# A ResNet block on one Trainium2 core: another written-out order of the same instructions, and nine more constant matmuls in its opening

## The chip, the core and the metric

The kernel runs on one core of a Trainium2 chip. The metric is the device time of one execution in microseconds (us); the number of the kernel before is the median of three runs. The profile is of one further execution, with its own time. The engines are TensorE (PE, with its weight loads PEld beside it), VectorE (DVE), ScalarE (ACT), GpSimd (POOL) and SyncE (SP), which issues most DMAs.

## What is computed

```python
B, C, HW, E = 2, 512, 64, 1152
h = conv3(_silu(gn(x, g1, be1)), w1)        # group norm of 4 groups, silu, 3x3 convolution 512 -> 512
emb = _silu(t_emb) @ w_emb
h = h + emb.reshape(B, C, 1, 1)
h = conv3(_silu(gn(h, g2, be2)), w2)
return x + h
```

Everything comes in and goes out in bfloat16. x is 2 x 512 x 64 x 64.

## The kernel before

The 512 channels are four blocks of 128 partitions (ct). An image is split into two chunks of rows, so that two layers, two images and two chunks give eight chunks, c = 0 to 7. Chunks 0 and 1 are image 0 in layer 1, 2 and 3 image 1 in layer 1, 4 to 7 the same in layer 2. A chunk has four units, one for each block of output channels: `u20` is chunk 2, output block 0. The convolution is done with transformed rows: for a chunk, `silu` (ACT) normalises and activates a block, `k`, `row` and `rob` (`rows_a`, `rows_b`; DVE with some ACT) form the planes of transformed rows, PE multiplies them by transformed weights into PSUM, ACT copies PSUM out (`o`, `m`, `b` in names), DVE recombines (`S`, `A`, `s`, `d`, `y`). The planes of chunk c+1 are formed while the units of chunk c run. So at the start of a chunk PE needs the last planes that DVE made (`rob13`, `rob23`, `rob33`, `rob53`, `rob63`).

Group norm of layer 2 is folded: `gn2_0` and `gn2_1` are chains of small DVE operations with one small matmul group in them; they use PSUM bank 7, which a `p5` group of a unit uses next. `emb` is a chain of its own: five matmul groups (`emb.0` to `emb.4`) each behind its load, then a DVE copy from PSUM (L1105).

**The opening.** Chunk 0 needs the statistics of x first. For each block ct, `stats0` (named `st0ct` below) takes the half x[0,ct,0] (`x0ct`) and the half x[0,ct,1] (`x1ct`). Block 0 uses four batch-norm statistics on DVE (L1125) for one half; blocks 1 to 3 use PE for it: eight matmuls of ones (128x260) and a Gram matrix of 17 matmuls (128x128), whose diagonal DVE sums (L1194). For the other half, each block has eight ones matmuls on PE and a square on ACT (2.1 us with its accumulator), and ACT reads the ones' sums from PSUM. Then `gn_chain` (L452 on) has a small group of fp32 matmuls, some DVE operations and a power on POOL, and gives scale and bias. Then `silu0ct`, `k0ct`, `row0ct`, and PE begins the convolution with the groups `o.0` to `o.23` (three 128x512 matmuls each): `o.6ct` to `o.6ct+5` are those of block ct. After them come the units `u00`, `u01`, and so on.

Two PE groups compute nothing that is used: `warm` is 11 matmuls of a constant tile of ones (128x512) in one step, and `fill` is a list of steps with one such matmul each. Both write PSUM bank 5 and depend on nothing but that bank:

```python
mm([(Ps(5, 0, [[1, 512]]), cone, wide, True, True) for _ in range(CFG["warm"])], "warm", chain=False, ...)
for i in range(CFG["fill"]):
    mm([(Ps(5, 0, [[1, 512]]), cone, wide, True, True)], "fill", chain=False, slack=0.0, slow=1.0)
```

**What sets the order.** `Plan.op` records each step with its engine, a cost, and the steps it depends on. `Plan.emit(ORDER)` then issues the steps in the order that the string ORDER spells (two characters for a step). Each engine runs its steps in the order in which they are issued, and so does each DMA queue; semaphores carry the dependencies. PE steps of the convolution are chained in program order; the statistics, `emb`, `gn2`, `warm` and `fill` (`chain=False`) may stand anywhere among them that their dependencies allow. Stores of the units wait for GpSimd's accumulating DMAs (`oa`), loads stand in SP's queue between such stores.

Of the kernel before, what the change touches and what calls it, by code (L numbers as in the profile page):

```python
# [165 lines left out]


ORDER = (
    "0E09000B0A2T0C0G0F0D0c010H020304050607080b0I160a130R0Z140X0g0S0Y150d0f0e0T0h1817190i0j0U0k1A0l1B0K1C2M1D0m0n1u0L"
    "0o2J0V0W1E0v0M1N1X3C1F0O1G1Y0p1Z0y0J1r0r1a3K1b1_0q1H201Q0N1c2c221d0s211e1I0t1f23241g4g0_1h3E251J0u2U261i271j0w28"  # L170
    "1K291k3F0x100Q0z120-2A3D1L1l2B1M1m1O1n2C4L111P1o1R2f1S4T3H1p2D1q1x2F1s3L2E1t1y1v2G1w1T2e2P2H2i2I3G2K1U2Q1-2L0P2N"
    "2W2O1V2X1z2l2Y1W2m3g2V2Z2R2n2b4O2h2d2o2S2p3a2a2q3X4N2r3M2s3N3h2g4M2t3i3O2u3P2v4U2k2w2x3Q2j2y3R2_2z3S3Z3j3d2-3k3u"
    "303T5P323v3U4V313w4Q3J5H4X3x4W3y3I3V3z4P333-4Y3_343l374Z423c3m3543366L3W443Y4a453b465J4S4h4k4738485K5Q493e394q3r"
    "4b3n4r3o4e4B4s5I4c4t4R3f4u4m4v406D4n4A4w414x4f4j6Y4-5R4_4d6M505T3p6Z513q525L6a535U547u556F5V5S5c4l3s5X4i5d7v5e4C"
    "6E5f7w5h5W5i4D4G4o5jB74EB85k4p3A4F5l5M4H5m5n3t5Z4I5Y5o566G8y575r4z6N5s4y5a5tB9583B5u5b5w6P5x595C5N5y6O5A6Q5z5BBB"
    "5-5v6RBN8z5_5g7h6S6I605D616b4J6T5E6H6c6U6d8l8-6e6XBA6W6g5q6h6iBFBCBP6j6kBD5p6l6mA06n626sBO6VBG636t6JBE5O6KA14K6u"
    "A25F6vB46x646y6w6z6-65686_7071BRBH727666B5BJ6777D56f6978DDBQ7PBIBT796A6o7Q6pBS7A7RB6DE737BBU7S6r5G7TBL7CBK7D7UBM"
    "7V7W7x7X747Y7Z7y7aD67E7b6q7z7c7F7d75DG7-7eDF7f7G80D781827gDH7i8384D985Ee86DJ87DL8C7H8DDI7I7j8E7JD27K8F7l888H7k8G"
    "8I8J8K8m7m8L8M8ND39p8O7n8S7L8T897p8U6B7M7_7o8VDN8A8W8Q7q8a8XD4D88n8Y8PDB8Z8o8_8bDA8p909qDMDC7r918q928BAt947s6C95"
    "9697988r998R9ADK9B9G7t7O8c9HEf8s9IDP9J8tEm9L8d9M9N9O8w8f9P9Q9R8e9S8x9W8g8u9XEg8h939Y9C9ZDOEi8i9D9r9aEuEh9F7N9bAu"  # L180
    "DR9cDQ9s9d9tA39UEn8vA49K9u9TA59ECr9e9vA69V9fA89xA9A7AA8jAB9gACAD9wAE9kAFAK9hAGAHAL9y9jAMEkEoAvAN9iEjAPEpAQAxElCs"
    "ARAS9-ATAUAVAWAa9lEvAbDS9zAX9mAcAyAYAdAw8kAeAzEO9_AfAIA_AgAiA-AhAJBVAjB09nBWEwAZCtBXB3AkBYB2BaBbAoBcAlBdAOBeBfCv"
    "AnBgBhBlCuAmBmBnBjBoApBiBtBZBuBpCwAqBkBvEyBq9oBwEbGJB1ByBzCQEqB-B_CREcC0GBC1CxExC2CTEdC3BxC6CUCzC7C8C4C9EsCCCAEr"
    "CDC5CyEtAsCEE-CVC-CFFxEzDTBrGLDUC_GDGKE_CGDVCSBsEPCWD1DWGCD0DYDZDaDbCBDcDdDgDeDfGFEQDjCXCHDkDlCYG8DmDrGNDhCZCIDs"
    "HhGECaGRG9DtCKCbERGMDuCLCJCcESDwFyDxDyCdGADzD-CeETD_E0E1CME4HUE5E6DoE7DnEAGHDiCNCfEBDXEUArGPE2ECGGDvEVEDGSHjEWF0"
    "GTCgGOE3F1GIChE8EXF2DqFzF3CiDpGQF5CjEaF6F7GVF8F9EEE9FAHpFBFCFEFGHVHlFHFIFJEFHxFOEYHiFPCkF_GUFQEGFLFREZEIFTEJFUEH"
    "FVG0FWFFFXFYF4GWFZFaEKFDFdFeHrFfFgHkFjG1FKELClGXFkFbF-HqFSFlGYJ6FMFcFmHtFhCOG2GZCPCmHnGaCnHmGbG3GcHzFNHyI3FnG5Ge"
    "GfJ7GgHsG7GhGiG4GnGjGmGkGlFiHWGpJ8GqHoGrGsHuGxFoEMGyHvGuKNGoGzFpGtCpG-HYI4FrHwFsH0G6H1H2ENH3H4CoHZH5H6H7FqHAHaHB"
    "FtHCHDH-HGG_HXFuHHGdGwKPHII5KOHbHEHJCqHcI6IBH9GvHKICHdNMH8IDHgJ9HfIENLIGHFIHIIIJIKI7ILIMHLINIRIQISH_ITHPIUHMIZIP"
    "I0IOIaHOHNI9IbIWI1IVIcIFI8I2HeIeJAIfHQIgIhFvIiIjIkIlIXHRIoInIpJCIqIAIdIrIuIYImJDIvIsJBIwJEItKQIxJGJSJLJFJTJUJHIy"  # L190
    "JJJVKRJXJYJZIzJaJbJcI-FwJdMvJeLeJiKTJjLfJkJlJIJqKSJ0JrKUOzI_JsJ1JKJtLgJfMxO-J2KVJvJwJgJxJhJyMwKXJzJ-JWJ_KWK0JnK3"
    "K4JuJMK5K6JmKbK9K1KYKAK2KaK7KBLhKCKZKjKcJNKkJoKDKlJ3LiKmJpJOKoKpKqK8KrKsKnKtKuLkKvKxKzMyJPK-HSK_L0KEL5LlL6LjLmL7"
    "KFKIOiL8OjKwJQLAKHNHNGLBLoLCKGLDLELnQBLFKyLGJRLHHTLKLLOkLpNJLMLNLQLrLROxL1L2KJLSMzQALTLsL-L4L_L9M_LIM0M-LJM1N0Pv"
    "LUM3L3PwM4LOM5KdM6N1M7M8LPM9J5MAJ4MEMFKeMGMHLVMMLqNKMCMNMDLWMOLZKKLXMPN2MBKLMRLYMSKfMTMUM2MVN3MWMJMXPxLtMIMYLaMb"
    "KMMcMdMeMhN6MiMQMLMjMZN4MkMaMKNNMfN7NOMlOyKgOlNPMgN8NQOHN5NSNTMmNUNVOmNWLbNXNYNZOIKhNbMnNcMqOKOnNdMoOoR5RMMpNFNe"
    "KiLdNgNhMrQ8NiNjNkNlNmOpLcNnNRNrNsMsNtOqNuNvLuNaNwQ9NxNyOrMuN-OLLvN_O0O1OsO2O3O4LwO5O_NfOMOJLxNoP0ONOwP1NzNpP2Nq"
    "O6P4OtP5P6PyP7O7OOP8P9PAOPPBLyPDO8PzPELzPFRKO9PGN9OAR7PIR6P-PJOCPKPLNAOBPMPNP3POOvPPMtPTPCPUPVPWP_PXPQPYPZRLODPa"
    "PcPHPdPePfQ0PgOEPhPiSZPRPjQ1QCPSOFPkQDOuTlPbQESHNINBQFQ3R8QHPlSIQIOGQJQKQLQMQ2QNQOQQPmNCQRPqPnQSQ5PoQTQ4PpQVSXQW"
    "QPQXQ7QYQZQ6QaR9QbQcQgSJQhTkQiNDQjQkQlPrQmQGQnQpQURNQqQrRBPtQoQsQtQuRAQvQwQdPsRCROSYNERPRDQeQxRQRERRW7SKRFRTPuRU"
    "QfRVRWRXRGSWRYTTRZRaRJSLRcRHRdTVRIReTiUfRfSNRhRiSMRjW6RkSORlRmRnQyRoSPRsRtRbUhRuTjRvSRRwRxRSRyQzRzR_TUS0SQR1S1S2"  # L200
    "S3Q-S4S5S6SUR0UgSaQ_SbRgSSScRpXJR2SdSfSVR-R3SgShOQSiORSjS7OSRqSkSlSmOTRrSoOUSpS8SnSqOVS9SrR4OWSASDStUvSuSvOXSwSB"
    "OYSxOZSyOaSCSzObSTS-T2UwS_T3OcT4OdT5OeOgT6OfSeT7OhSET8TWT9TBUuTCTDTET1SFTFTGTHT0TITmTATnTJToTXTpTKTrTsTtTLTuTvSs"
    "TwVrTZTxSGTyT-TzTaT_TYTbU0TMVsUiU1TcTdU3U4UxU5TPU6TeU7TNU8U9TfTOVtUAUEUFUjTgUGUHUIUJUKThULW4UNUOTqTQUPX1UQUBURUS"
    "W5UTUlUUTRUyUMUkUzUVUmU-UDX2UnU_UCU2V1UpVuV2V3V4UoV5V6TSV7UWX3V8VAVBUqVCUXXGVvUtVDUYVFVGVHUsVIUZYFVJVKV9VLVMUbVQ"
    "VxVRVNVSVTVwVUVVUaVWVyYDVXVZVEVaUcYEVbVzVcVdV0VeVfUrUdVgVYW8ZnVPW9VhV-WAV_X4WBVOXIWDW0WEWFWGViWHWIX5WJWKWMW2WNVj"
    "YGWOZUb0X7WPVkXHWRWSX6WTWLWUWVW1YVWWZSUeWXWYVmVnWcX8WdVlWeZmWfW3WZWgWhWiVoZTWjWlX9WmWnWCWoXBVpWpWQWqYXWrXAWkWsXK"
    "WaXLWtXCXMXEYHXNYYXFXPXQXRWbXSZVXTXUYJXVXWXYWuXZXXYIXaZkWvahVqXbYKXdYWXeXDXfXgXhYLXiWwajXjaiXkYNXoWxXpXqYMWyXrXs"
    "XtXlWzXuYOXvXxXyYPXOXzX-ZWX_W-cLY0Y1Y2YZYQW_YaXcZlYbY3XnYcZXXwYebyZYbwYfYgYhXmYiYjYRYkYlYnYmY4YoZZYpY5YqbxZaY9Ys"
    "Y6YtYuZcYvY8YwdbYxZbY7YyYzZ1Y-azYAZ2Z3Z4Z5akZ6Z7ZeYBZ8ZAZBY_ZCZDX0ZdZEZFZGYdZ0ZHZ9ZoYTZpZfZIetZqYrYCZJZrala_ZtZu"
    "ZiZvZwZxZKZyZzbza-Z-ana0Zga1aoa2Zsama3ZOapZLa5cDa6a7aqZNa8a9aAarZMaBaCZ_ZjaGesaHasaIaJaDaKauaLaMaNa4aPcCaQZPaRb-"  # L210
    "aSaTaUaVaWavZQb1aFaOb2c0b3aXb_b4c1b6aEb7b8b9c2bAatbBbCbDaYZRbFbGc4bHdTaZbIc3adbKaabLbMdcbNc7bOacbPbQabbRbVbEbWYS"
    "dUbXaebYbZbabSbbbcaxbeafbfbdcKbgc6bhbibjc8bkblcMbmYUcNcOcHcPbUcQb5cRcSaycTcVbTcWagcXcEcYcZbncacbcccgcdchZhcicjbo"
    "ckcUclcmcJcncIbJbpcpcqcrc5brcsctcucFbqcvcGcwbscBczc-cAc_c9d0d1awd2btd3d4d9dAdBdCcfcobudDdEdFceekdGcxdddYdedfdadg"
    "d5dhdVdidZdIdjdkeldXdmd6dWdndocydHdpdqdrdlbvdsdtd8dxdydKdudzd-d7d_e0dLe1e2e4dJdNe5e6e7dMdOe8e9dPeAeBeEeFeGeHdRe3"
    "eIdweJeKeLeCdveQeReSemeTeNepeUeVdQeMeWf_eDeXdSeueYeveweZexg0eyePezene-e_erf1f0eOf2f3eqf4gveof5f6ebf7f8fCeaf9fDfE"
    "ecfFfGfHeffIeeedfJfLfMegfNfOfPfQfRfSeifKfVehfWfXfAejfYfTfZfBfafbfcfhfUfefifjfdfkflfmfnfffofsg1fqg2g3ftfpg4g5g6fw"
    "g7fvfug8fggAg9gBfxgCgDgEgFgGfrgHgLgIgMfygNgOfzgPgQgJf-gRgSgUgKgTgVgWgXgYgZgagbgegcgfgdggghgogjgpgkgsgrgqglgugmgt"
    "gngwgigxgyg_gzh0g-"
# [1172 lines left out]
```

## Time and profile before

| | us |
|---|---|
| runs: median (lowest to highest) of 3 | 460.74 (459.73 to 462.39) |
| the profiled execution's own time | 462.31 |
| its span, first to last instruction | 460.5 |
| busy in the span: PE, DVE, ACT, POOL | 448.6, 436.9, 402.8, 57.8 |
| granted TensorE clock, mean | 0.992 |

In the profile, times are from the span's start. A row of a timeline gives start, length and, in brackets, the idle time of that engine before it and what released it. A table by windows gives each engine's busy time in a stretch, and PEclk, the share of full clock that TensorE was granted there. All engines issue in order, so with ORDER each instruction of the trace can be matched to its step.

### The profile page before, as it was taken

Reading aid. Unit: us, or ns where it says so; the run is one execution under the profiler, and the core shown is the slowest. Engines: PE = TensorE matmul, PEld = TensorE weight load, DVE = VectorE, ACT = ScalarE, POOL = GpSimd, SP = SyncE. Lnnn points to the kernel's source line nnn. Section 1 sums busy time; section 2 is a strip of 40 time slices with the busy share of each in tenths; the row PEclk is TensorE's granted clock in tenths of the full one; section 3 lists DMA queues with packets and bytes.
Section 4 is the critical chain, followed back from the end, with each engine's and each line's share of the span. In section 5 each row is a group of like instructions: output and inputs, shape, how many; then the busy total and the mean of one; then the engine's idle time right before and its main releaser. Section 6 shows DMA issues by size and latency. Waiting matters only on the chain. (4 is left out here: it accounts for less than half of the span.)

```text
span 460.5 us, 8098 instructions
## 1 busy us (share of the span) xinstructions
PE 448.6 (97%) x2891; PEld 282.0 (61%) x2891; DVE 436.9 (95%) x811; ACT 402.8 (87%) x611; POOL 57.8 (13%) x82
## 2 busy tenths in 40 slices
...
PEclk9979999999999999999999999999999999999999
...
GB/s 322 398 243 71 124 238 47 141 255 214 165 175 212 122 190 224 149 243 220 257 231 231 357 177 218 190 225 231 176 238 164 268 227 252 164 186 121 165 109 93
DMA packets 43176, 92.49 MB, mean 201 GB/s; under 512 B 6400, under 2 KB 18048, under 8 KB 43136
## 3 DMA queue, kind: packets, MB, share of 16 engines
...
q8 instruction: 22, 0.36, 0.3%
q14 instruction: 18, 0.15, 0.1%
...
## 5 line engine op out<-in xcount | busy, mean ns | idle before, releaser
L401 PE MATMUL psum<-ar 128*128 128x256 f16 (+2 forms) x2771 | 429.6, 317 | 2.7 <-ACT ar L371 1.9
L348 DVE TENSOR_TENSOR ar<-ar 128x1024 f16<-128x1024 f16 (+7 forms) x630 | 413.0, 717 | 7.6 <-ACT ar L371 4.7
L401 PEld LDWEIGHTS <-ar 128*128 128x128 f16 (+1 forms) x2763 | 268.7, 98 | 159.9 <-issue 9.6
L371 ACT ACTIVATE ar<-ar 128x512 f16<-128x512 f16 (+6 forms) x186 | 186.9, 1041 | 24.3 <-DVE ar L348 23.3
L371 ACT ACTIVATE ar<-psum 128x512 f16<-128x512 f32 (+3 forms) x250 | 159.1, 681 | 21.2 <-PE psum L401 13.8
L371 ACT ACTIVATE ar<-ar,fs 128x2112 f16<-128x2112 bf16 (+1 forms) x32 | 68.8, 2154 | 3.5 <-DVE fs L494 2.8
L386 POOL DMA_DIRECT2D ar<-ar x26 | 30.8, 1207 | 217.9 <-DVE ar L348 190.7
L386 POOL DMA_DIRECT2D out_dram<-ar x15 | 18.7, 1244 | 58.6 <-DMA ar<-ar 41.8
L371 ACT ACTIVATION_READ_ACCUMULATOR ar<-psum 128x1 f32 x104 | 22.6, 217 | 0.0
L352 DVE TENSOR_SCALAR ar<-ar 128x520 f16<-128x520 f16 (+3 forms) x50 | 19.5, 402 | 0.0
L390 POOL MEMSET ar<- 128x65 f16 (+4 forms) x29 | 5.8, 270 | 93.6 <-DVE ar L348 48.8
L401 PEld LDWEIGHTS <-ones_bf 128*128 128x128 bf16 x75 | 7.7, 108 | 5.9 <-issue 3.3
L401 PE MATMUL psum<-fs,ones_neg 128*128 128x1 f32 (+3 forms) x36 | 5.4, 263 | 3.0 <-ACT ar L371 2.9
L401 PEld LDWEIGHTS psum<-fs,ones_neg 128*128 128x128 f32 x36 | 5.2, 214 | 4.3 <-ACT ar L371 3.7
L401 PE MATMUL psum<-ones_bf 128*128 128x512 bf16 x19 | 6.8, 536 | 1.1 <-DVE ones_bf L405 1.1
L371 ACT ACTIVATION_READ_ACCUMULATOR ar<-ar 128x1 f32 x36 | 7.2, 201 | 0.0
L401 PE MATMUL psum<-ar,ones_bf 128*128 128x260 bf16 x56 | 7.1, 275 | 0.0
L1125 DVE BATCH_NORM_STATS2 fs<-ar 128x6 f32<-128x512 bf16 x4 | 2.5, 680 | 3.7 <-DMA ar<-in_x_dram 3.7
L479 POOL TENSOR_TENSOR fs<-fs 128x1 f32<-128x1 f32 x4 | 3.0, 744 | 19.2 <-DVE fs L477 18.6
L1105 DVE COPY ar<-psum 2x512 f32<-2x512 f32 x1 | 0.7, 679 | 2.6 <-PE psum L401 2.6
L439 ACT ACTIVATE s_sb<-tparm 128x18 bf16<-128x18 bf16 x1 | 0.2, 218 | 2.9 <-DMA tparm<-in_t_emb_dram 2.9
L438 DVE CAST fs<-gparm 128x16 f32<-128x16 bf16 x1 | 0.2, 174 | 2.7 <-DMA gparm<-in_params_dram 2.7
...
## 6 DMA issues: line engine op xcount, KB each, us to landing
...
```

The source lines that it names most:

```text
L348: pl.op("DVE", 0.075 + 0.000521 * out.n, lambda: nc.vector.tensor_tensor(out=out.ap, in0=a.ap, in1=b.ap, op=op), regs(a, b), regs(out), name)
L352: pl.op("DVE", cost or 0.075 + 0.00026 * out.n, lambda: nc.vector.tensor_scalar(out=out.ap, in0=a.ap, scalar1=s, scalar2=None, op0=ALU.mul ...
L371: lambda: nc.scalar.activation(out=out.ap, in_=a.ap, func=func, scale=sc, **kw), regs(*rr), regs(*ww), name)
L386: lambda: eng.dma_start(out=out, in_=in_, **kw), regs(*r), regs(*w), name, lat=3.2 if sw else None, after=after, sw=sw, seq=seq)
L390: pl.op("POOL" if eng == "gpsimd" else "DVE", 0.08 + 0.0005 * out.n, lambda: e.memset(out.ap, v), (), regs(out), name)
L401: nc.tensor.matmul(out.ap, lhsT=lhsT.ap, rhs=rhs.ap, start=st, stop=sp, skip_group_check=True)
L438: nc.vector.tensor_copy(out=fs[:, GB:GB + 4 * CT], in_=gparm[:])
L439: nc.scalar.activation(out=s_sb[:], in_=tparm[:], func=ACT.Silu)
L479: pl.op("POOL", 0.85, lambda: nc.gpsimd.tensor_tensor(out=F(rs, n).ap, in0=N.ap, in1=F(NEGH, n).ap, op=ALU.pow), regs(N), regs(F(rs, n)), ...
L1105: pl.op("DVE", 0.6, lambda: nc.vector.tensor_copy(out=est.ap, in_=pe.ap), regs(pe), regs(est), nm)
L1125: pl.op("DVE", 0.61, lambda: nc.vector.bn_stats(out=q.ap, in_=e.ap), regs(e), regs(q), nm)
```

## The change

The number of `fill` steps goes from 8 to 17, and ORDER is another permutation: 2762 steps in place of 2753. No other line differs.

```diff
-    'fill': 8,
+    'fill': 17,
...
 ORDER = (
-    "0E09000B0A2T0C0G0F0D0c010H020304050607080b0I160a130R0Z140X0g0S0Y150d0f0e0T0h1817190i0j0U0k1A0l1B0K1C2M1D0m0n1u0L"
...
+    "0N000J0I2c0M0O0P0l010i0Q020k0g0h0p0j0304050607080R0m0o1C0n0a0q0b1D0r0s1F0t0u1E0c0L0v090A0B0w1G1H210x0T1I120U0d0V"
...
```

Spelled out by the names of the steps, the opening is this (g = the small fp32 group of a `gn_chain`; each number behind a name is the block):

```
PE before   warm, 8 fill, ones0, ones1, gram1, ones1, g0, g1, ones2, gram2, ones2, ones3, gram3, g2, ones3, o.0, g3, o.1 to o.23, u00
PE after    warm, 2 fill, ones0, 6 fill, ones1, g0, gram1, ones1, 3 fill, g1, 6 fill, ones2, gram2, ones2, ones3, o.0, g2, gram3, ones3,
            o.1, o.2, o.3, g3, o.4 to o.23, u00
ACT before  sq0, sq1, read0, read1, silu00, silu01, sq2, read2, sq3, read3, st10, silu02, st10, silu03, st10, silu10, w1_1, st10, u00o4
ACT after   sq0, read0, sq1, read1, silu00, sq2, read2, silu01, sq3, read3, silu02, st10, st10, silu03, w1_1, w1_1, silu10, u00o4
loads before  x10, x11, x01, x00, ld_ur0, w1_0, x02, x12, x03, x13, five ld_ur of 192 KB, st10, ...
loads after   x10, x00, x01, x11, ld_ur0, w1_0, x02, x12, x03, two ld_ur of 192 KB, x13, ld_ur, w1_1, ld_ur, st10, ...
DVE after   block 0's chain, diagonal 1, four of w1_0, k00, block 1's chain mixed with w1_0 and row00, rob00, block 2's chain, k01, row01, ...
```

(`sq` is the square, `read` the read of the ones' sums, `st10` statistics of image 1, `w1_1` the scaling of layer 1's next weights, `ld_ur` loads of weights.) Behind the opening, the chained PE groups keep their sequence; `emb`, `st1` and `gn2` matmuls move by one to four groups, and the steps of DVE, ACT, SP and POOL are interleaved anew through the whole kernel. The emb groups, for instance, stand at:

```
before  u00p3.1 emb.0 u00p2.2 ...   u00p1.3 emb.1 u00p3.3   u01p0.3 emb.2 u01p1.0   u02p2.0 emb.3   u02p1.2 emb.4 u02p1.3
after   u00p2.1 emb.0 u00p0.1 ...   u01p2.1 emb.1 u01p2.2   u01p1.0 emb.2 u01p1.1   u02p0.0 emb.3   u02p1.3 emb.4 u02p3.0
```

More of the change, by code (lines that the diff above doesn't have):

```diff
@@ L168 @@
 ORDER = (
-    "0E09000B0A2T0C0G0F0D0c010H020304050607080b0I160a130R0Z140X0g0S0Y150d0f0e0T0h1817190i0j0U0k1A0l1B0K1C2M1D0m0n1u0L"
[L170 to L218, printed above, removed]
+    "0N000J0I2c0M0O0P0l010i0Q020k0g0h0p0j0304050607080R0m0o1C0n0a0q0b1D0r0s1F0t0u1E0c0L0v090A0B0w1G1H210x0T1I120U0d0V"
@@ new lines @@
+    "0C0D0E150F0S0G2l0H0y1g1J1-1K0W1h3O1L0-1M1j1i0z1W0e1k2V281N0_3L1l1O0X101P1m182S291Z1n191o1p1B2B1q2A1Q110K2d1r2C1s"
+    "0Y132D4p1t141R2E1S162F1T173T3N2G1u1U2H1w2I1V1A3M1X0f2J1v1Y2K1x1a2o2L1b4U0Z1y1z244c2m1_2M202O2n222N232P3U252Q2r2R"
+    "272T262f2U1c3p2e2g2W2Y2h2X1d2i2Z2a2u4V2b2v1f2w1e2x2k3V4W2y2p3q2z2q3r2-3Q2s3g2_3X305Q3Y2j312t3P32333W3Z343S3b4d4X"
+    "353R3a363j375Y3c38413B3e423A4e3s3i3l433t443f4f39453h3d464g473C4Y4h483k4B6U3u3m5R4C3o3v4D4q4E3D3G4F4i3F4j4G3E4k4Z"
+    "4H4l4I3H4z5Z4-5T4o3I4t4_3n5049515a5S3w3-5b523x4m534a5c4s546M5d574n4J585e3J4w4A596V4v5A7q3y5f5B3z5C5V6h5D5g5E6i5l"
@@ new lines @@
+    "4K5h6N5m4b6j3_6W5n4L6O5o814M5q4u5r4NBG5s824P5t404O6Y4r5u4Q5v835U5w4R4x5x5-6X55955_6P565W5k605F4y615G5i633K5HBH64"
+    "4S5I655X5j665K6Z5J676a5L6b68BI6c5p695M6Q6A6k6g5N6l6d6RBK6m6fBW6n966p6qBJ6rBO6s626tBL6u6v5zBM6w6_6C97BN705y6e6SA9"
+    "6B71BXBP4TAA72AB7475766T776D78BY79BD7ABQ7B6E7F73BS7GBZBa6F7HBbDM6GBE7IDE6HBc7J7N6IBd6x7YBR7K7ZBF6o6J7a7L7b6yBTDN"
+    "7M7cBU7C7d84BV7e7D6z7f7O857g7h7i5O5P6-867j7k7E877l897m8u7P8A8BDG8C7n8D7oDO7p8EDI8F7r8GDQ8L7QEn8MDB8NDCDP7sDF8O8H"
+    "DU7TDS8Q6K7u8R7S8S8T7RDR8U8V7v8I8W8XEo8b7tDT6L8c7w7U9y8d8e7x8v7V8f8K7y8g8J7z8h88DD8iDH7_8j988Z7-99DWDK8Y9A80EpDJ"
@@ new lines @@
+    "9B8k8wDV9DDL8P9E8a9F9GEq9H8y9I9J9K8l9P8z9Q8x9R8-B08m9SEr8n9U9V909W8p9X7W9YDY8o9Z9a8_9L9b9f9z8q9g9hEv918r949i9M9-"
+    "9j9CEt9k9TA09c9l9_B19mA1AC92EsAD9OF29dAEA2F1939nAFC-9o9NAHA47XAIAJAK9eALAMANA3AOAT9pAGAUA5DXAV9t9q8tAWB2AYDZAZAa"
+    "B4AbAcAdB39sAeAfAQDaAjA7Ew9rAkEuAPAlA6C_B58sAm9uAnAoF3B69vASAhApA8DbAXARAqB7AgBeB8F4ArBfAiExBgB9AsBBBhEyD0BjBCBk"
+    "BlAtBmBnBoEzBpBqAxAuGKBuBvBwF5EXAwBxC0EkAvD2C1BrAyBsGSC2Bt9xC3D3AzC5ElC6CZC7BAD1ByC8C9BzCACaEmCDCBCCF7CFC4CGE_CH"
+    "CIBiE-CLD4GMF0F6CMGUD5CECNGLD6CJF8COGOA_DcCcGWGTB_9wDdD7DeCPCdDADfEYCeCbB-DhCfDiCKGaDjDkDlG4DmD8DnGVDoCQDsGNDtDu"
@@ new lines @@
+    "EZGHDvA-D9CgChGID-CiCRDqD_DrGJCUCjCSE0CkEbDgE1ClDpGPDxE3CmEcDwE4E5CTE6EaE7GcE8E9EdEAGQEDEEGYEFGREGEeEJEHCVEKE2Gb"
+    "HqELEfECCWEMEBDzF9DyENGXFAG5EIHrFBGZEiFCHdFEGdCnEgFFFGFHGeFIG6FJEOFKHyFLFPCoFQGgFRFSEjFXHsCpG8FOFYG7FMFZFUG9HtJH"
+    "FaESEPFcFDCqFdGAFeEQERFfCrEhFgFhFNCsFiHuFTFjHeFmGfI4FnFoCtETFpGhFsFtGCEUCXFbFuGBFkFvJFFWFlFVGiFqCuGFHzH-GjFwGkFr"
+    "CYGlHwGnGDGoGpFxGqGrHfGsHvGtGuI0GyHxGzGGG-G_H4GEGwKWI5GvCvJGHgH5GxFyH_H6H1HhH0H7ICF_I1H9I6HAHiHBF-HCFzHDCyHEGmI2"
+    "HFHGHjEWIDHJG0HKEVHLHMHPCwHkG1HQKYH8I3HlHRIEH3I7HSH2HICxHpIKHHKXCzHmILHNHoIMHTJIINI8G2HnIPIQHOIRISITIUIGIFIVIWIX"
@@ new lines @@
+    "HUIaIbIZIcIIIdIYIiHVHYIjIfI9IeIHIkHXHWIJIOIAIlHZJJInIoIpIqIrIhHaIsItIgIuIvIxJLIyLnIzIwI-JKJ1I_JMLpJ2ImJ0LoJNJ3KZ"
+    "JPJ4JOJbJUJQJcJ5JRJdKaJ6JeJTJgJhJiJ7JjJkG3JlKcN2JmJnKbJrJsJtKdJuHbJzJAJSJ-KeN4J8J_N3KfJpK0J9KgLqK2JBK3IBK4K5K6K7"
+    "K8KhNUK9KCKkKDJoKEJvKFNVKiKIJfKjKJJqJwKKKAJyKBKLJVLrKsKlJxJWKtJCKuK1LsKvKGLtOrKxKMKyKHKzK-HcK_L0LuL1L2L6KNL7P6L8"
+    "L9JXLELvNSKOL4LFL3LxKRLGOsLwKPLHKQJYLJKwLKL-OtLLP4LML5LNLOLBLPLAL_LQNTLTN5LULzLVLWLZLyJDLaJZLIKSLbN6LcJaM7LCM8Km"
+    "LSQ4QKM9LRN8MAJELDQJN9MCMDMEKTMFRWMGMHKnLXMIMJN7MNM0LdMOMPLYMQNAMVMKNBMWOuNCMXLeMYNGMaMLMbLiLfMcMdMMMeNFP5MfMgLg"
@@ new lines @@
+    "MhMkLhMlP7NDMmMBMnMqNEMSKUMoMrLjNRNOQ2MRMsMZKoMtMjMTMiNWNHMUMuNXKpOvNYMpNZLkNbMvNcKVNdNeOQNfOxNgNhMwNiNkQ3ORKqMy"
+    "NlMzOTOyNmMxKrNnOzM-LmNpNqNrNsM1NtNuNvM_NwN-NaN_M2O0NjO1OUO2OwO3O4N1O5OVM3REO7RFO8O9O-OAOBOCM4ODOENxO_RGP8RVOSM5"
+    "P9NoN0OWO6NzPAP0PBOFNyLlPDPEQ5PFM6PGPHOGPIPJOXQIPKOYP1PMQ6QHOHPNNIPORTOIPPPCQ8OKPRPSP3PLPTPUPVQ9PWOLPXP2PYPcOJPd"
+    "PePQPfPgQ7PZPhPiPjOMSQPlNPSRPmQAPnPoPpQBONPqPrPsQCQLPtOONJQMSSTuRHPaQNQDQOQFShQQQRPkQSOPQTPbQUQVRIQWSiNKQXQZQGRU"
+    "QaPuQbSTQcRKRJQeQfQgPvQhTeQiSfQjRLPzQkQlQpPwRMQqQrNLQsQYQtV4QuQEQvQwPxQyNMQzPyQ-Q_ROR0QPR1R2P-QmR3RXQdRYRNWFQ0R4"
@@ new lines @@
+    "RZNNV3QxRPTcRaRRRcSURdReRfWGRgQoRhRiRjQnRlSgUoRSNQRkRmP_SWRnRbSVTdRoSXRqRrRQQ1RsSYRtRuOZR5RvRwRxUpR_S0S1SZS2S3R6"
+    "S4S5S6OaSaS8RAS9SATrRpR7SBSCSDSbSER9SFSjSdR8TtRySkObSlRBSmSeRCS7SoSpSqOcR-SrSGSsStOdRzSuSvSxOeSwOfSHSySzV1OgSIS-"
+    "OhSMOiSJT0T1TsOjT2ScSLT3T4SKT5OkT6OlUqXRT7OmOnTBOpT8OoTCOqTDSNTETFTfTGTHV2TIT9SOTKTLTMTATNTORDTPTQSnTRTJTvTwTSTx"
+    "TgTTTyT-T_TUU0U1U2S_TiV-U3SPU4U5ThU7U6TjU8TYTkV_TVU9UrTmUATlUCUDUETqUFUGXSUHTWTnUIUJTXUNToUOUPTzUQTpW0URUsYgUSUT"
+    "UUUWTZUXUYUZWEUaUBUbUcUuTaUdUKV5UtV6UVXAUvV7UMXBUwV8ULUeUxVAVBW1VCUyVDVEVFUfXCVGWDVHVJUzVKTbU_W2VLZvVMUgVOVPV0XP"
@@ new lines @@
+    "VQVIVRVSW3VTVUVVUhYMVZVaXQW4VbUiVcVdU-V9VeVfUjVgUkViW5VjVNVkVlUlW6YNVmVnVoVWVpWHW8UmVhWIVXVYWJVqW7WKXDVrWMWNWOWP"
+    "WQW9WRWSWTVsWVXEWBWWWXYeVwVtWYXGVuYOWaWbXFVvWcWdb8WeWUWAWfZbWgWhVxWlWLWmWnWiWoZdWpXHWqVyWrWZWsWCWuZcWvXIWwUnWjWx"
+    "WtWyWzXJW-W_YPXTXKYfXUXLXVXNXWYQXOXYXZXaWkXbXcXdXMcTXeX0XfYSXhXgYRXiasYTXjaqXXVzX1XkXmXlZuXnYUXoX2ZeXpXqXrYVXsXt"
+    "arX3XxXyXzYWX-X_X5Y0X6Y1ZwYXX4Y2Y4XuY5YZY6Y7Y8Y9ZfYAX7YBYib9YjYYX8Y3YkZgYlZhYCcUc3YnXvYoYpc5ZiYqYrYsXwYtYuc4YwYa"
+    "YvX9YxZjYDatYyZtYzZkY_YEb7Z0Z1ZlZ2YIZ3Z4YFb6YmZ5Z6ZAZmYGZBZCZDZnYHZEZFauZGZoZHZJZKZLdlZMYJZNZOZPZ7ZQZxawYKY-Zyav"
```

9 lines of the change are left out of this document (added).

## The prediction

> **What bounds the kernel now.** I read the page's first two parts, then the timeline of PE in the opening, the table by microseconds with the clock, the waits, and last each engine's steps, matched with ORDER.
>
> ```profile
> PE 448.6 (97%) x2891; PEld 282.0 (61%) x2891; DVE 436.9 (95%) x811; ACT 402.8 (87%) x611; POOL 57.8 (13%) x82
> ...
> PEclk9979999999999999999999999999999999999999
> ```
>
> PE is busy for 448.6 of 460.5 us, so at most some 12 us can go while its work stays, and DVE is only 12 us behind it. The one visible dip of the clock is in the third slice. The timeline of PE around it:
>
> ```profile
> 17.20 1.24 PE L401 MATMUL psum<-ar 128*128 128x128 bf16 x17
> 21.30 0.83 PE L401 MATMUL psum<-fs,ones_neg 128*128 128x2 f32 x6 [2.87 <-ACT ar L371]
> 21.99 1.06 PE L401 MATMUL psum<-ar,ones_bf 128*128 128x260 bf16 x8
> 22.89 1.19 PE L401 MATMUL psum<-ar 128*128 128x512 f16 x3
> 23.95 1.44 PE L401 MATMUL psum<-fs,ones_neg 128*128 128x2 f32 x6
> 25.26 11.10 PE L401 MATMUL psum<-ar 128*128 128x512 f16 x39
> ```
>
> PE idles 2.87 us until ACT has read the ones' sums of block 2 (g2 at 21.30), and the convolution proper (o.1) begins only at 25.26. The table by microseconds gives the clock (columns: PE, PEld, DVE, ACT, POOL busy with counts, clock, DMA):
>
> ```profile
> 22.00:23.00 1.00, 1.00 (x11) 0.86 (x11) 0.95 (x4) 1.00 (x2) 0.00 (x0) 1.00 1.03 385
> 23.00:24.00 1.00, 1.00 (x5) 0.15 (x2) 1.00 (x7) 0.75 (x5) 0.47 (x1) 0.59 0.86 332
> 29.00:30.00 1.00, 1.00 (x4) 0.38 (x3) 0.97 (x4) 1.00 (x2) 0.00 (x0) 0.50 0.00 0
> 30.00:31.00 1.00, 1.00 (x6) 0.45 (x5) 1.00 (x2) 1.00 (x3) 0.00 (x0) 0.99 0.00 0
> ```
>
> A mean of 0.59 puts the fall to half at about 23.2, and 0.99 the return at 30.0: 6.8 us at half clock, 3.4 us of work lost at most. Weight loads in that stretch start every 0.43 us, while 47 matmuls fill 30:40, 0.213 us each.
>
> What else waits:
>
> ```profile
> PE psum L401 <- ACT ar L371: 4.8, 5, 2.9
> ...
> DVE ar L1105 <- PE psum L401: 2.6, 1, 2.6
> ```
>
> Of PE's 4.8 us only 1.9 lie behind the opening, and its windows 30:140, 140:270 and 270:420 leave 0, 0.72 and 1.92 us idle. DVE's are 4.03, 0.52 and 2.96; 2.57 of the first are the wait for the last emb matmul at 74.6. So from 30 to 420 both engines are full. Their matched steps show who is ahead: at the chunk starts DVE's last planes come just in time (rob13 0.6 us before PE uses it at 98, rob23 0 at 155, rob53 and rob63 0.05 at 314 and 364, the last weights and planes of chunk 7 0 at 418). A gain in the opening is kept only if DVE comes forward too.
>
> **The nine fills.** One takes 0.216 us at full clock (0.43 at half), 1.94 us in all, and no step waits for their result. They cost nothing where PE would idle. Bounds: 0 to 1.94 us at full clock, 3.9 at half.
>
> **The opening, step by step.** Durations are those of the same steps before: ones 1.0, Gram 1.2, g 0.8, silu 2.1, square with accumulator 2.1, read 0.5, k 0.65, row 0.7, w1_0 0.55 to 0.95.
>
> Loads: the first four move 2.2 MB at 410 to 425 GB/s and DVE's first statistic starts at 8.62 with the fourth, x00. Now x00 is second; by the bytes (estimate) it lands at 6.1, and the last of the four, x11, at 8.6. PE: warm and two fills to 6.4, ones0 to 7.4, six fills to 8.75, ones1 to 9.75, g0 (DVE's sums ready at 9.25) to 10.55, gram1 and ones1 to 12.8, three fills to 13.45. ACT: sq1 waits for x11, 8.9 to 11.0, read1 12.85 to 13.35, then silu00 13.4 to 15.5 (before: 14.78 to 16.93). PE: g1 to 14.2, six fills to 15.5, ones2, gram2, ones2 to 18.6, ones3 to 19.6.
>
> ACT: sq2 to 17.6, read2 at 18.65 to 19.15. Block 1's chain on DVE now stands behind k00 (16.2), w1_0 and row00, so silu01 starts about 20.25, 3.4 later than before. o.0 follows row00 at 20.05 (before 22.89), g2 20.7 to 21.5, gram3 and ones3 to 23.7, o.1 to o.3 to 25.6, g3 (read3 ends at 24.95) to 26.4, and o.4 starts at **26.4 against 29.05**. PE has no idle time over about 0.5 us here, so I take full clock. Next, silu01 20.25 to 22.35, sq3, read3, silu02 24.95 to 27.05, two st10 to 31.3, silu03 to 33.4 (before 32.19). DVE: row01 done at 27.3, in time for o.6 at 27.7; row02 at 31.4 for o.12 at 31.55; k03 33.4 to 34.1, row03 at 36.1, while PE would want it at 35.4. So o.18 starts at **36.1 against 38.86: PE gains 2.75 us**, a 0.7 us wait included. rob01 ends at 43.1, just before PE needs it.
>
> That is dense in choices; with x00 0.7 us later, or the clock lost for 3 us, it is 2.0 or 1.3.
>
> **What DVE gains.** k03 starts 0.7 later (33.4 against 32.69), but 1.47 us more work lies ahead of it: 0.8 gained. At the emb copy, 0.69 us more DVE work lies ahead, so DVE arrives at 72.0 + 0.7 - 0.8 = 71.9; emb.4 has 2.62 us more PE work ahead of it, 1.94 of it fills already counted, and ends at 74.56 + 0.68 - 2.75 = 72.5. The wait falls from 2.57 to 0.6, and DVE is 0.8 + 2.0 = **2.8 us** ahead.
>
> **Later.** I summed the durations of DVE's steps ahead of each boundary's last step, new less old: rob13 -1.1, rob23 -1.1, rob33 0, rob53 +0.4, rob63 0, the last of chunk 7's planes +0.6; the copy that frees the bank of gn2_0 +0.8. With 2.8 gained, DVE allows PE 3.9, 3.9, 2.0 (at gn2_0, 171 us), 2.8, 2.4, 2.8, 2.2. The smallest, 2.0, is what lasts; I put 0.1 back for slack there (0.05 us was left). On ACT the margins into PE come out at about 0 to 1 us from 95 to 250; its 4 us of waits for DVE and PE between 100 and 156 shrink as those come earlier, which I count as covering it; if not, up to 2 us of PE waits return. The last ten us behind the final A matmuls keep their chain, 0.
>
> **Sum.** 462.31 - 2.1 = 460.2 on the profiled execution; the same off the median, 460.74 - 2.1 = **458.6 us**.
>
> [...]
>
> **Rivals.** (1) *DVE doesn't come forward*: emb's five loads share one buffer, each waits for the group before; moved later by one to four groups they may hold the copy at 74.6 as before. DVE then has 0.8, less 0.6 at chunk 7: 0.2 us gained, **460.5**. For: every boundary is at 0 to 0.6 us. Against: emb's loads land in 2.7 us, its groups stand 6 us apart. (2) *The clock falls anyway*, somewhere before o.4: half of 6.8 us, 3.4, against 2.75 - 0.7 gained: **462**, 461.4 if part falls on waits. Against: no long idle time is left. (3) *Slower*: ACT becomes the bound, through late loads. In SP's queue the loads of layer 2's weights and of h stand closer to their use: with 5 us to land, about eight of the loads used between 105 and 232 us (w2_02, w2_22, w2_23, w2_30, a23, a42) come out at -1 to 1 us ahead where they had 2 to 5. ACT is busy for 127.1 of 130 us in 140:270. Its margin is used up at about 0, each further us of wait then delays PE by one; it is slower than before once the loads cost over 2.1 us, and at 0.6 us for each of eight, 4.8 in all, the time is **463.4**. Against: 96 and 192 KB loads land in 2.9 and 3.1 us, not 5. (4) *More than forecast*: PE's 2.6 us of waits from 140 to 420 go in part with the new interleaving, 1.7 of them: **456.9**. That the fills fail to fill, and stand before needed groups, costs at most 1.94 and is within (1).
>
> **Chances.** Forecast 0.45 (457.6 to 459.7), (1) 0.17, (2) 0.07, (3) 0.16, (4) 0.15. A measurement can tell about 0.5%, 2.3 us: faster means under 458.4. Of the forecast 0.21 lie there, with (4) 0.36; same 0.24 + 0.17 + 0.07 = 0.48; slower 0.16. The range leaves out most of (3) and a third of (4): 456.2 to 463.0.
>
> **What would show it.** Right: no half clock behind the first 6 us; o.4 near 26.4 and o.18 near 36; the emb copy's wait under 1 us; PE waits at 171 us. Wrong: a clock under 1.00 between 10 and 40; o.18 after 38; waits of ACT for loads of weights or h, by several us between 100 and 260; a total PE idle over 3 us behind 30 us.

## The result, and the profile after

| | before | after |
|---|---|---|
| runs: median (lowest to highest), us | 461.46 (459.63 to 463.93), 22 runs | 462.86 (462.42 to 463.25), 22 runs |
| the profiled execution's own time, us | 462.31 | 462.44 |
| its span, us | 460.5 | 460.7 |
| mean granted clock | 0.992 | 0.998 |

The ratio is 1.0037, with a 95% interval from 1.0023 to 1.0051: 0.4% slower. That is within the half per cent that was called no change, but the interval lies wholly above 1, and the forecast, 458.6, was a gain. 462.86 still lies in the range that was stated, 456.2 to 463.0; that is due to the width of the range and not to the sum. The order before spreads over 4 us from run to run (its runs gather near 459.6, 460.6, 462.3 and 463.8), and in its profiled run TensorE's clock was at half for 6.83 us; after the change the runs keep within 0.8 us. So two things are to be explained: what took the spread away, and what it cost.

The page after, the lines that answer to those of before:

```profile
PE 447.4 (97%) x2900; PEld 281.6 (61%) x2900; DVE 438.1 (95%) x811; ACT 401.6 (87%) x611; POOL 58.3 (13%) x82
...
PEclk9999999999999999999999999999999999999999
```

TensorE is busy for 1.2 us less although it has nine matmuls (1.9 us) more: the dip in the third slice is gone. VectorE has the same 811 instructions and is busy for 1.2 us longer. The timeline of TensorE in the opening after, and the clock there by microseconds (the columns are those of before):

```profile
19.40 0.83 PE L401 MATMUL psum<-ar 128*128 128x512 f16 x3 [0.25 <-DVE ar L348]
20.07 0.72 PE L401 MATMUL psum<-fs,ones_neg 128*128 128x2 f32 x6
...
24.73 0.72 PE L401 MATMUL psum<-fs,ones_neg 128*128 128x2 f32 x6
25.32 9.51 PE L401 MATMUL psum<-ar 128*128 128x512 f16 x42
35.19 5.05 PE L401 MATMUL psum<-ar 128*128 128x512 f16 x22 [0.36 <-DVE ar L348]
```

```profile
23.00:24.00 1.00, 1.00 (x6) 0.44 (x5) 1.00 (x5) 1.00 (x5) 0.04 (x1) 1.00 0.82 293
...
29.00:30.00 1.00, 1.00 (x7) 0.40 (x5) 1.00 (x4) 1.00 (x3) 0.00 (x0) 1.00 0.00 0
```

The 2.87 us of idle in front of g2 are gone, the clock is 1.00 where it was 0.59 and 0.50, o.4 starts at 25.3 (before 29.05) and o.18 at 35.19 (before 38.86). TensorE is 3.7 us ahead of the profiled run before, and still 3.3 us ahead just before 151 us. The end is the same to 0.2 us. The timeline of TensorE from 150 us, rows with idle time in front of them, shows where the lead goes:

```profile
151.90 6.85 PE L401 MATMUL psum<-ar 128*128 128x512 f16 x45 [1.05 <-DVE ar L348]
159.09 10.08 PE L401 MATMUL psum<-ar 128*128 128x256 f16 x66 [0.34 <-DVE ar L348]
170.12 10.12 PE L401 MATMUL psum<-ar 128*128 128x512 f16 x57 [0.60 <-DVE fs L469]
```

These are the last planes of chunk 2 (rob23) and the copy that frees gn2_0's bank. All three wait for VectorE, and behind the third TensorE is 1.1 us ahead. Further waits follow at 229, 270, 363, 396 and 418 us, 0.34 to 0.67 each; those at 229, 270 and 396 are for ScalarE, and only the one at 270 was there before (1.04 us). Behind the one at 229 TensorE's lead is 0.4 us. By kind, from the list of waits after (total, times, longest):

```profile
DVE ar L348 <- ACT ar L371: 6.7, 7, 2.4
...
PE psum L401 <- DVE ar L348: 2.9, 6, 1.1
PE psum L401 <- ACT ar L371: 2.3, 5, 0.7
...
DVE ar L348 <- PE psum L401: 0.8, 1, 0.8
DVE ar L1105 <- PE psum L401: 0.4, 1, 0.4
```

TensorE's wait for ScalarE has shrunk from 4.8 to 2.3 us and the emb copy's from 2.6 to 0.4, and TensorE waits 2.9 us for VectorE, where it was 0.2 before. VectorE's own waits for ScalarE have grown from 4.7 to 6.7 us.

### The profile page after: what moved, and what is told of

The parts are those of the page before. It is cut to its first block, busy times and chain, and to the rows that moved or that the text cites. A ratio compares the mean times of both kernels' runs of the same rounds, so it can differ in the third digit from the quotient of the medians.

```text
span 460.7 us, 8086 instructions
## 1 busy us (share of the span) xinstructions
PE 447.4 (97%) x2900; PEld 281.6 (61%) x2900; DVE 438.1 (95%) x811; ACT 401.6 (87%) x611; POOL 58.3 (13%) x82
## 5 line engine op out<-in xcount | busy, mean ns | idle before, releaser
L348 DVE TENSOR_TENSOR ar<-ar 128x1040 f16<-128x1040 f16 (+7 forms) x630 | 414.4, 719 | 10.4 <-ACT ar L371 6.7
L371 ACT ACTIVATE ar<-psum 128x512 f16<-128x512 f32 (+4 forms) x250 | 160.0, 685 | 26.0 <-PE psum L401 9.5
L401 PE MATMUL psum<-ones_bf 128*128 128x512 bf16 x28 | 8.7, 465 | 1.1 <-DVE ones_bf L405 1.1
L401 PE MATMUL psum<-ar,s_sb 128*2 128x512 bf16 x9 | 2.7, 377 | 0.0
```

The costliest lines, as they stand in the source:

```text
L348: pl.op("DVE", 0.075 + 0.000521 * out.n, lambda: nc.vector.tensor_tensor(out=out.ap, in0=a.ap, in1=b.ap, op=op), regs(a, b), regs(out), name)
L371: lambda: nc.scalar.activation(out=out.ap, in_=a.ap, func=func, scale=sc, **kw), regs(*rr), regs(*ww), name)
L401: nc.tensor.matmul(out.ap, lhsT=lhsT.ap, rhs=rhs.ap, start=st, stop=sp, skip_group_check=True)
```

## The experiments

Two theories of the loss stood at the start. **VectorE's lead**: TensorE's gain lasts only as far as VectorE has the same lead, and the new order behind the opening spends it. **Something local**: the fills, or single steps put badly in a queue. Each kernel was timed beside the kernel before on its own chip.

**old_nine_in_gap.** The order before, with nine fills in the gap:

```diff
- ones3, gram3, g2, ones3, o.0, g3, o.1 ...
+ ones3, gram3, 9 fill, g2, ones3, o.0, g3, o.1 ...
```

> The old order, with nine more fill steps put only into TensorE's 2.87 us gap ahead of block 2's small fp32 group (g2); nothing else moves. Theory 1 (the half clock decides the old kernel's time, and its runs at 459.7, 460.6, 462.3 and 463.9 are such with none, one, two or more windows of it): no half clock behind the first 6 us, every run at 459.7 to 460.0, ratio to before about 0.996. Theory 2 (the old kernel is bound by VectorE, so that an earlier TensorE is worth nothing, and its spread has another cause): the same spread and median as before, 461.5, although the clock stays full.

Measured: 459.61 us (459.32 to 459.84), before 460.86 (459.41 to 463.97), ratio 0.9966 [0.9945, 0.9988]. The timeline of TensorE in this kernel:

```profile
18.44 2.12 PE L401 MATMUL psum<-ones_bf 128*128 128x512 bf16 x9
21.37 0.83 PE L401 MATMUL psum<-fs,ones_neg 128*128 128x2 f32 x6 [0.81 <-ACT ar L371]
```

The idle time is 0.81 us in place of 2.87, the granted clock is 1.00 from 22 to 24 and from 29 to 31 us and 0.999 on average over the run, and all twelve runs lie where the fastest runs of before lie. So the spread of before goes when the gap is filled, and with it the half clock that the profiled run has behind the gap. The mean clock of a run does not tell its group by itself: the runs of before under 460 us have means from 0.993 to 0.999, so a lowered clock alone did not make a run slow. In the profiled runs before and after, part of it lies behind TensorE's last matmul (455.3 and 455.1 us): the clock is at half from 460.1 and from 459.15 us to the end. How many stretches of half clock the other runs of before had, and where, is not shown. The old order without the gap takes 459.6: that is the measure for the new one, which is 3.2 us slower.

**new_without_nine.** The changed kernel without the nine added fills:

```diff
-    'fill': 17,
+    'fill': 8,       (and the nine steps out of ORDER)
```

> The new order without the nine added fills (the three ahead of g1 and the six behind it go; TensorE then idles some 0.8 and 1.5 us there). Theory 1: the gaps are too short for the clock to fall in most runs; the time stays at 462.5 to 463, with a spread of its own up to 465 if it does fall in some. If the nine cost their own 1.94 us on the path: 461. Theory 2: 462.9 whatever the clock does.

Measured: 462.97 us (462.24 to 465.13), ratio 1.0043 [1.0021, 1.0065]. The median is that of the changed kernel. The fills cost nothing; in the new opening they can at most narrow the spread (one of the twelve runs without them took 465.13).

**new_open_old_rest and old_open_new_rest.** The new order up to VectorE's k10, then the old one; and the reverse:

```diff
- ORDER: after
+ ORDER: after up to k10, the remaining steps in the order before     (new_open_old_rest)
+ ORDER: before up to k10, the remaining steps in the order after     (old_open_new_rest)
```

> The new order up to VectorE's first step for chunk 1 (k10, about 42 us), then all remaining steps in the old order; 17 fills. Theory 1 (the loss lies in the new interleaving behind the opening, between 75 and 240 us): about 459.5 to 460, with the full clock. Rival (the loss lies in the new opening itself, which delays block 1's activation by 3 us and leaves VectorE 1.2 us more idle): 462.5 or more.

> The old order up to the same step, with nine more fills in the 2.87 us gap, then all remaining steps in the new order. Theory 1 (loss in the new interleaving behind the opening): 462 to 463. Rival (loss in the new opening): 459.7 to 460.

Measured: 459.83 us (459.54 to 460.24), ratio 0.9976 [0.9956, 0.9996]; and 463.65 us (463.26 to 464.07), ratio 1.0052 [1.0031, 1.0074]. The loss lies behind the opening. In front of the new rest, the new opening is worth 0.8 us (463.65 against 462.86). In front of the old rest it ends no earlier than old_nine_in_gap, although TensorE's o.18 starts 0.68 us earlier (35.37 against 36.05). That does not yet show that a lead of TensorE is worth nothing, since TensorE loses it at 51 us to a load for emb.1:

```profile
51.06 0.59 PE L401 MATMUL psum<-ar,s_sb 128*2 128x512 bf16 x2 [0.89 <-DMA ar<-in_w_emb_dram]
```

**new_to_120 and new_to_177.** The new order up to unit u12 (120 us) or up to u22 (177 us), then the old one:

```diff
+ ORDER: after up to u12p4.0, the remaining steps in the order before    (new_to_120)
+ ORDER: after up to u22p4.0, the remaining steps in the order before    (new_to_177)
```

> The new order up to TensorE's first group of unit u12 (about 120 us), the rest in the old order. Theory 'VectorE's lead': by 120 us the new order has spent VectorE's lead on waits (0.76 us for emb.5 ahead of u01s, 0.4 for w2_00, 0.87 ahead of u03y) and stands 0.8 us behind the old order without the half clock; as that has no slack at chunk 2's start, the time is about 460.4. Theory 'local queue order' (only the steps placed in front of chunk 2's last planes and of the copy for gn2_0 cost): 459.0 to 459.6, since TensorE is 0.5 us ahead there.

> The new order up to TensorE's first group of unit u22 (about 177 us), past chunk 2's first planes and gn2_0, the rest in the old order. Both theories: most of the loss is in, 461.2 to 462.0. If it lies later (the wait for ScalarE at 229 us and what follows): 460.5 or less.

Measured: 460.54 us (460.39 to 460.70), ratio 0.9993 [0.9972, 1.0015]; and 461.83 us (461.62 to 462.13), ratio 1.0004 [0.9983, 1.0024]. With 459.83 and 462.86 at the ends, the new order loses 0.7 us up to 120, 1.3 from there to 177 and 1.0 behind it (roughly, since these kernels ran on different chips). No single place holds it. With the steps matched, VectorE is behind old_nine_in_gap by 1.0 us from 144 us to the end in new_to_120, and by 2.2 us from 200 us to the end in new_to_177: as much as their times are above its 459.61 (0.9 and 2.2).

**new_three_undone.** The changed kernel with the steps in front of its three largest waits put back:

```diff
- u13A, rob23.4            gn2_0's matmul group and its copy as after
+ rob23.4, u13A            group right behind u21B1, copy in front of n1_3.3
```

> The changed kernel with three steps put back as in the old order: VectorE's u13A behind rob23.4 and not ahead of it, the gn2_0 matmul group three groups earlier on TensorE, and its copy from PSUM two steps earlier on VectorE. Theory 'local queue order': the waits at 152 us (1.05) and 170 us (0.6) go or fall to under 0.3 each, and the time falls by 1.2 to 1.5, to about 461.5. Theory 'VectorE's lead': VectorE has no less to do ahead of the next boundaries, so they take most of it back; the waits shrink, the time falls by under 0.5.

Measured: 462.52 us (462.43 to 463.48), ratio 1.0028 [1.0003, 1.0052]. The wait for gn2_0 went, but 0.58, 0.53 and 0.33 us stood at the start of chunk 2, 0.31 at rob33 and 0.48 at rob53: under 0.4 us of the 3 came back, and the runs overlap with those of the changed kernel (462.42 to 463.25). The waits move with VectorE; for these three steps the local theory falls.

**emb_later.** new_open_old_rest with three emb groups moved, since emb.1 waited 0.89 us for its load there and VectorE 1.26 us for emb.4:

```diff
+ u01p2.0 emb.1    u01p1.0 emb.2    u02p1.0 emb.4
```

> The new opening with the old rest (459.8 us), and the emb groups placed anew on TensorE: emb.1 two groups later (its load landed 0.89 us late there), emb.2 one later, emb.4 two earlier (VectorE waited 1.26 us for it); the loads of emb.2 follow emb.1. If TensorE's wait at 51 us and VectorE's at 72 us are all that took back the new opening's 0.7 us on TensorE and 1.3 on VectorE: 458.8 to 459.1. If another wait takes it (a load of emb that now comes late, the copy at 102 us): 459.5 to 459.8.

Measured: 459.47 us (459.10 to 459.97), ratio 0.9959 [0.9937, 0.9981]. Beside the 459.61 of old_nine_in_gap that is no clear difference: VectorE then waited 0.68 us at 81.4 for ScalarE, which has no idle time from 21 to 90 us. TensorE's wait at 51 us is gone, and TensorE comes to chunk 2 0.3 us ahead of old_nine_in_gap. There it waits for VectorE, and the lead is gone:

```profile
152.91 3.35 PE L401 MATMUL psum<-ar 128*128 128x256 f16 x23 [0.45 <-DVE ar L348]
```

So this small lead of TensorE, without one of VectorE, was worth nothing.

**vector_twice, tensor_twice, scalar_twice.** These ask directly which engine sets the time of the changed kernel: some steps of one engine between 112 and 152 us are executed twice, with the same values.

```diff
             self.ops[i].fn()
+            if i in (502, 570, 638, 706):        # k20, k21, k22, k23            (vector_twice)
+            if i in (584, 601, 617, 621):        # u12 p4.0, p5.0, p1.0, p3.0    (tensor_twice)
+            if i in (615, 865, 963, 964, 955):   # u12m0, w2_11, w2_20 (2), w2_13 (scalar_twice)
+                self.ops[i].fn()
```

> The changed kernel, in which four of VectorE's steps between 112 and 143 us, the multiplications by 4 that open a block's planes in chunk 2 (k20, k21, k22, k23; 0.72 us each there, 0.64 us apart from their neighbours), are executed twice in a row: 2.6 us more VectorE work, the same values. Its own time is 462.9 (the changed kernel as measured). Theory 'VectorE sets TensorE's start of chunk 2': TensorE waits there for VectorE already (1.05 at 151.9, 0.34 at 159.1, 0.60 at 170.1), so all 2.6 us stand in front of TensorE: 465.5, or 464.4 if the later waits of TensorE (0.57 to 0.67 at 229, 270, 363, 396 and 418) take up half of it. Rival 'TensorE's own work sets the end, these waits are incidental': the 2.42 us that VectorE waits at 324 take it up, 462.9 to 463.4.

> The changed kernel, in which four TensorE groups of three 128x512 matmuls (the first group of p4, p5, p1 and p3 of unit u12, from 120 to 133 us, 0.67 us each) are executed twice in a row; each begins its accumulation anew, so the values stay: 2.67 us more TensorE work. Theory 'VectorE sets TensorE's start of chunk 2': TensorE's waits for VectorE at 151.9, 159.1 and 170.1 (2.0 us together) take up that much, and 0.7 stays: 463.6. Rival 'TensorE's own work sets the end': 465.5. If ScalarE or VectorE, which wait for TensorE's results, fall behind as well, it is 465.5 too, and then VectorE shows new waits for PSUM between 120 and 150.

> The changed kernel, in which five of ScalarE's steps between 136 and 152 us (one copy out of PSUM of unit u12 and four scalings of layer 2's weights, 0.53 to 0.61 us each) are executed twice in a row, the same values: 2.7 us more ScalarE work, in a stretch (128 to 155) in which ScalarE has no idle time. Theory 'VectorE sets TensorE's start of chunk 2': the next waits of ScalarE behind it (0.32 at 155, 1.16 at 175.7, 0.80 at 177.6) show that it has some room; VectorE's steps that read ScalarE's copies get up to 2.7 later there, but stand behind others in its queue: 462.9 to 463.9. Rival 'ScalarE is the engine behind VectorE's lateness': all of it is seen, 465.5.

Measured, beside 462.86 of the changed kernel:

| | time, us | ratio to before | more than the changed kernel |
|---|---|---|---|
| vector_twice | 466.40 (466.22 to 466.72) | 1.0107 [1.0085, 1.0130] | 3.5 for 3.0 of work |
| tensor_twice | 463.27 (462.91 to 463.98) | 1.0048 [1.0029, 1.0066] | 0.4 for 2.7 of work |
| scalar_twice | 465.08 (464.79 to 465.89) | 1.0080 [1.0057, 1.0104] | 2.2 for 2.7 of work |

The timelines of VectorE and TensorE in vector_twice (the code's lines are two further down):

```profile
113.22 1.48 DVE L354 TENSOR_SCALAR ar<-ar 128x2145 f16<-128x2145 f16 x2
```

```profile
155.34 6.86 PE L403 MATMUL psum<-ar 128*128 128x512 f16 x45 [3.56 <-DVE ar L350]
```

A k with its repeat takes 1.48 us, where one took 0.72: the four add 3.0, more than the 2.6 expected. VectorE has no wait over 0.3 us between 105 and 310 us to take that up, so the wait at the start of chunk 2 grows from 1.05 to 3.56 us and everything behind it is later. With the steps matched, VectorE falls 3.0 us further behind the changed kernel by 152 us, stays there, and loses another 0.6 at 311 us, in a wait for ScalarE that the changed kernel does not have: together the 3.5 of the table. TensorE's extra work, in contrast, goes into its waits at 152, 159 and 170 us; of those only 0.26 us at 170.6 is left. ScalarE's is mostly seen: VectorE waits 0.97, 0.38 and 0.67 us for its copies from 152 to 159, and TensorE's wait at chunk 2 grows to 2.10. In this profiled run TensorE's clock then falls to half, from 153.1 to 156.6 us:

```profile
153.21 7.05 PE L403 MATMUL psum<-ar 128*128 128x512 f16 x36 [2.10 <-DVE ar L350]
```

```profile
154.00:155.00 1.00, 1.00 (x5) 0.56 (x4) 0.62 (x3) 1.00 (x4) 0.00 (x0) 0.50 0.00 0
```

That is not what makes the 2.2 us: the two runs with a mean clock of 0.999 took 464.79 and 465.37, the four at 0.992 to 0.994 took 464.88 to 465.89. So between 112 and 152 us VectorE binds the changed kernel, with ScalarE close behind it, and TensorE, at 97% busy, does not.

**block0_first.** A try at a better opening, the old rest behind it: block 0's chain first on all three engines, so that VectorE and ScalarE gain a lead too.

```diff
- loads x10, x11, x01, x00     ACT silu00, silu01, sq2, ...      PE ..., ones1, g0, g1, ones2, ...
+ loads x10, x00, x01, x11     ACT silu00, ..., silu01, ...      PE ..., 3 fill, g0, ..., 2 fill, g1, ..., 4 fill, g2, ...
```

> The order before with 17 fills and the opening written out anew: loads x10, x00, x01, x11; on VectorE, TensorE and ScalarE block 0's statistics, scale, silu, k and row planes first (its small matmul group ahead of block 1's ones, its silu ahead of block 1's read, the squares of blocks 2 and 3 behind silus), fills where TensorE waits (8 behind warm, 3 before block 0's small group, 2 before block 1's, 4 before block 2's); emb.1, emb.2 and emb.4 as in emb_later; the rest as in the order before. By its queues (estimate) o.18 starts at 33.4 where it starts at 36.0 without half clock, ScalarE is 3 us ahead and VectorE 1.8. Theory 'a lead lasts only as far as VectorE and ScalarE have it too': 457.8, since both have it. Rival 'another wait takes its place in the first 100 us' (ScalarE has no idle time from 20 to 90 us, and VectorE waits for it at 81): 459.4, as old_nine_in_gap and emb_later. Slower than 459.8 if VectorE's steps for block 0 wait for loads that now come later.

Measured: 464.53 us (464.04 to 465.03), ratio 1.0066 [1.0043, 1.0089]: a miss. The timelines of VectorE and of TensorE show why:

```profile
20.70 0.29 DVE L1194 SCALAR_TENSOR_TENSOR ar<-psum,ident 128x128 bf16<-128x128 f32 x1 [1.97 <-ACT ar L371]
```

```profile
26.09 0.83 PE L401 MATMUL psum<-fs,ones_neg 128*128 128x2 f32 x6 [1.96 <-DVE ar L1194]
26.79 10.84 PE L401 MATMUL psum<-ar 128*128 128x512 f16 x48
40.38 4.83 PE L401 MATMUL psum<-ar 128*128 128x512 f16 x21 [2.75 <-DVE ar L348]
```

ScalarE's read of block 2's sums now stands behind silu01 and ends at 20.57; VectorE waits 1.97 us until then, and four times 0.43 to 0.45 us for GpSimd's power or a small matmul group, 3.7 in all. Its own planes of block 3 come late and o.18 starts at 40.4 in place of 36.05. The rest of the order is the old one, and from there to the end TensorE and VectorE stay 4.2 to 4.7 us behind old_nine_in_gap. The time is 4.9 above that kernel's. What VectorE loses in the first 35 us is still missing at the end.

## Why the prediction was wrong, point by point

**The nine fills: right.** They cost nothing (462.97 without them, 462.86 with them).

**The clock and the opening: right, and a little small.** No half clock from 6 us to TensorE's last matmul (1.00 from 6 to 455 us); o.4 at 25.3 where 26.4 was forecast, o.18 at 35.19 where it was 36.1, since silu00 to silu02 came 0.4 to 1.1 us earlier than worked out. TensorE gained 3.7, not 2.75. The second rival, that the clock falls anyway, did not come. The profiled run before had its clock at half for 6.83 us, from 23.19 to 30.02, where its gap of 2.87 us had ended at 21.30. That the half clock varies from run to run is seen in the means alone: from 0.988 to 0.999 over the runs of before.

**"What DVE gains", 2.8 us: a little small where it was measured, and for the most part not a gain of the new order.** The emb copy was forecast for 72.5 with 0.6 us of wait. VectorE's timelines, before and after:

```profile
74.59 0.68 DVE L1105 COPY ar<-psum 2x512 f32<-2x512 f32 x1 [2.57 <-PE psum L401]
```

```profile
71.58 0.68 DVE L1105 COPY ar<-psum 2x512 f32<-2x512 f32 x1 [0.44 <-PE psum L401]
```

It came 3.0 us earlier, with the 0.7 us of work moved in front of it a lead of 3.7. But in old_nine_in_gap it starts at 71.78 with a wait of 0.33, also 2.8 us earlier. So three quarters of the lead were nothing but TensorE's half clock, handed on to VectorE. An order compared with a run that has the dip is credited with what any run without it has.

**"Later", the step that failed.** The prediction took the 2.8 us as kept and subtracted only the work that stands ahead of each boundary. The steps at its boundaries, matched, show how much of it was left (the lead is the earlier start plus the work moved in front of the step, as in the prediction):

| VectorE's step | rob13 | rob23 | gn2_0 copy | rob33 | rob53 | rob63 | last of chunk 7 |
|---|---|---|---|---|---|---|---|
| started before at, us | 97 | 155 | 171 | 207 | 313 | 363 | 418 |
| allowed by the prediction, us | 3.9 | 3.9 | 2.0 | 2.8 | 2.4 | 2.8 | 2.2 |
| started earlier by, us | 3.9 | 2.9 | 1.1 | 1.1 | 0.7 | 0.4 | -0.3 |
| lead of VectorE, us | 2.8 | 1.8 | 1.9 | 1.1 | 1.0 | 0.4 | 0.3 |

At 97 us the prediction was right; the 2.8 that it took as lasting had shrunk to 1.9 at gn2_0 and was gone at the end. In chunk 2 it also summed a plane that TensorE does not wait for in the new order: the one it waits for at 151.9, rob23.4, has 0.6 us more work in front of it in the new order and came only 1.2 us earlier (151.16 for 152.37). VectorE loses time on its way, as its timeline after shows (all its waits from 75 to 125 us):

```profile
76.74 3.37 DVE L348 TENSOR_TENSOR ar<-ar 128x1024 f16<-128x1024 f16 x5 [0.76 <-PE psum L401]
94.75 1.98 DVE L348 TENSOR_TENSOR ar<-ar 128x768 f16<-128x768 f16 x4 [0.40 <-ACT ar L371]
103.79 1.23 DVE L348 TENSOR_TENSOR ar<-ar 128x2048 f16<-128x2048 f16 x1 [0.87 <-ACT ar L371]
```

The last of these was 0.48 us before, the first two are new: VectorE now waits for results of TensorE and ScalarE that have not come forward as far as its own steps. The wait at 324 us has grown from 1.66 to 2.42. And VectorE is busy for 438.1 us where it was 436.9. Matched step by step, VectorE's lead of the changed kernel over old_nine_in_gap at equal work done runs like this:

| VectorE in the changed kernel at, us | 6 | 16 | 48 | 72 | 85 | 96 | 106 | 144 | 182 | 264 | 365 | 452 |
|---|---|---|---|---|---|---|---|---|---|---|---|---|
| lead, us | 2.6 | 1.4 | 1.2 | 0.9 | 0.2 | -0.5 | -0.9 | -1.1 | -1.4 | -2.1 | -2.5 | -2.5 |

It ends at -2.5, where the spans, 460.7 and 457.8, differ by 2.9. The spliced orders fall along it: beside the 459.61 of old_nine_in_gap, the new order up to 120 us costs 0.9 where the lead is -0.8, and up to 177 us 2.2 where it is between -1.1 and -1.4 here, and -2.2 from 200 us on in new_to_177's own trace. That a lag of VectorE reaches the end whole was shown by vector_twice, new_to_120, new_to_177 and block0_first; that a lead of TensorE alone is worth little by emb_later, and that a delay of TensorE costs little by tensor_twice. What is not shown: the splices put back the order of all engines at once, and the repeats were tried between 112 and 152 us only. So how much of the loss begins in ScalarE's order, on which VectorE waits 2 us more than before, and which of the many moved steps costs each tenth, stays open.

**The sum.** From 458.6 to 462.86 are 4.2 us. The first step, 462.31 - 2.1 = 460.2, missed the profiled 462.44 by 2.2: VectorE's lead. Taking the same 2.1 off the median was worth another 1.6 and was a mistake of its own: the 2.1 was worked out against a run with the dip, and filling the gap alone is worth 2.7 to that run (462.31 to 459.6), but 1.1 to the median of 460.74. The last 0.4 is the changed kernel's median above its profiled run.

**The rivals.** That VectorE doesn't come forward (460.5) was the right mechanism, given for another reason: no emb load was in the way in the changed kernel, and it lost its head start, not the emb copy's wait. That ScalarE becomes the bound through late loads did not come in that form: TensorE's waits for ScalarE fell to 2.3 us. But scalar_twice shows that ScalarE's time is nearly as dear as VectorE's between 136 and 152 us, a cost that the prediction took to be covered by ScalarE's 4 us of waits between 100 and 156 us. That the interleaving takes away TensorE's waits was wrong: from 140 to 420 us they grew from 2.6 to 5.4 us.
